# A cached attention decode on one core: three additions of a pair's weighing become one sum over eight tiles

## The chip, the cores and the metric

The kernel runs on one core of a Trainium2 chip. The metric is the device time of one execution in microseconds (us). The engines are called as in the profile: PE is TensorE, PEld its weight loads, DVE is VectorE, ACT is ScalarE, POOL is GpSimd, SP is the engine that issues nearly all transfers.

## The reference

Two layers of the same kind run one after the other, for a batch of two with one token each (D = 448). A layer is an attention over a cache and a gated feed-forward network, each behind a layer norm and with a residual. All data is float32.

```python
def _A_ref(x, k_cache, v_cache, wq, wo):     # B 2, H 16, Sk 4096, Dh 256
    q = (x @ wq).reshape(B, Sq, H, Dh).transpose(0, 2, 1, 3)
    scores = jnp.einsum("bhqd,bhkd->bhqk", q, k_cache) * (Dh ** -0.5)
    p = _softmax(scores, axis=-1)
    o = jnp.einsum("bhqk,bhkd->bhqd", p, v_cache)
    return o.transpose(0, 2, 1, 3).reshape(B, Sq, H * Dh) @ wo

x = x + _A_ref(_layernorm(x, axis=-1), A_k_cache, A_v_cache, A_wq, A_wo)
x = x + _B_ref(_layernorm(x, axis=-1), B_W_gate, B_W_up, B_W_down)
x = x + _A_ref(_layernorm(x, axis=-1), A_k_cache, A_v_cache, A_wq, A_wo)
x = x + _B_ref(_layernorm(x, axis=-1), B_W_gate, B_W_up, B_W_down)
```

## The kernel before

A *pair* is one head of one batch entry. There are 32 pairs in a layer, numbered u = 0 to 31, and the second layer goes through them backwards. A pair has 4 MB of keys and 4 MB of values. One large buffer in SBUF, `arena`, holds three pairs, the head weights and, later, the feed-forward weights. Most pairs come as one transfer of 8 MB for keys and values together; the first few and the last few of a phase come in pieces. The query and output weights of three heads come as one transfer ahead of every sixth pair.

All these transfers are issued by SP in a fixed order, from a list called `pending`. When the program releases a piece of the buffer (`release`), `pump` issues the next transfers of the list for which the buffer has room. A transfer therefore waits for the work that last used its place: an 8 MB transfer for the value tiles of the pair three before it, a weights transfer for the output projection of a head. SP's queue is in order, so a transfer that waits holds up those behind it.

For a pair u the work goes as follows.

- `score` (L379): PE multiplies the keys with the query, 32 matmuls into one of two PSUM banks, `raw`.
- `score_copy` (L387): DVE copies the scores to `found_s`; `score_turn` (L392): PE turns them with four transposes.
- `softmax_max` (L397, L399): DVE takes the maximum over each partition, POOL over all partitions. `softmax_exp` (L404, L407): ACT makes the probabilities `probs`, POOL adds up their sums (L411).
- For most pairs (u = 0 to 28 in the first layer, 5 to 28 in the second, 53 in all) the values are weighed on DVE and ACT. `weigh_rows` multiplies 24 of the 32 value tiles of 256 columns with their probabilities in one DVE instruction (L462); ACT does the other eight (L466). `fold` (L456) then adds the upper half of the tiles to the lower half, in place: 16 tiles, then 8, 4, 2 and 1, the last into `row`. The other pairs are weighed by PE (L439, L430).
- `out_turn` (L486): PE adds `row` over the partitions and scales it with `ri` (L415). ACT copies the result to `oT`, and `project` (L279) multiplies it with the output weights. `query` (L337) makes the query of the next head.

The order of the DVE instructions is the order of the program. `scores_beside(u)` writes out how the scores of pair u and the end of the weighing of pair u - 1 interleave: before, the additions of 16 and 8 tiles stand in `weigh_rows`, right behind the multiplication; that of 4 tiles stands behind the copy of the next scores; those of 2 and 1 stand behind the maximum. After the last one, the value tiles of pair u - 1 are released, and with them the place of a further pair.

Of the kernel before, what the change touches and what calls it, by code (L numbers as in the profile page):

```python
# [11 lines left out]
AX = mybir.AxisListType  # L12
RED = bass_isa.ReduceOp

B, D, H, S, DH, F = 2, 448, 16, 4096, 256, 1792
# [74 lines left out]
def two_layers(  # L90
# [10 lines left out]
    nc = tc.nc  # L101
# [63 lines left out]
    def release(*key):  # L165
        units.free |= units.grains(*at_of.pop(key))
        pump()
# [50 lines left out]
    row = consts.tile([P, DH], F32, name="row")  # L218
# [102 lines left out]
    def attention(order, after, by_rows):  # L321
# [53 lines left out]
        def score(u, c):  # L375
            kt = get("k", order[u], c).rearrange("p (g n) -> p g n", g=G)
            half, j = c // 2, c % 2
            for g in range(G):
                nc.tensor.matmul(  # L379
                    raw[u % 2][32 * g : 32 * g + 2, :], q_of[u][:, j, 1 - half : 3 - half],  # L380
                    kt[:, g, :], start=(c == 0), stop=(c == NC - 1),
                )
            if ("k", order[u], c) not in after:
                release("k", order[u], c)

        def score_copy(u):
            nc.vector.tensor_copy(found_s, raw[u % 2])  # L387

        def score_turn(u):
            s = ps_s.tile([P, E, P], F32, name="small")  # L390
            for e in range(E):
                nc.tensor.transpose(s[:, e, :], found_s[:, e * P : (e + 1) * P], ident)  # L392
            s_of[u] = s.rearrange("p e (g r) -> p r e g", g=G)[:, :2]

        def softmax_max(u):
            mx = work.tile([P, 1], F32, name="mx")
            nc.vector.reduce_max(mx, s_of[u], axis=AX.XYZ)  # L397
            mx_of[u] = work.tile([P, 1], F32, name="top")
            nc.gpsimd.partition_all_reduce(mx_of[u], mx, P, RED.max)  # L399

        def softmax_exp(u):
            b = order[u][1]
            nm = work.tile([P, 1], F32, name="nm")
            nc.scalar.activation(nm, mx_of.pop(u), AF.Copy, scale=nsr[:, b : b + 1])  # L404
            p_of[u] = work.tile([P, NT], F32, name="probs")
            rs = work.tile([P, 1], F32, name="rs")
            nc.scalar.activation(  # L407
                p_of[u].rearrange("p (h e g) -> p h e g", h=2, e=E), s_of.pop(u), AF.Exp, bias=nm, scale=sr[:, b : b + 1], accum_out=rs
            )
            r_of[u] = work.tile([P, 1], F32, name="total")  # L410
            nc.gpsimd.partition_all_reduce(r_of[u], rs, P, RED.add)  # L411

        def softmax_sum(u):
            ri = work.tile([P, 1], F32, name="ri")
            nc.vector.reciprocal(ri, r_of[u])  # L415
            if added(u):
                r_of[u] = ri
                return
            r_of[u] = work.tile([P, 2], F32, name="ri2")
            nc.vector.tensor_scalar_mul(r_of[u], lead, ri)  # L420
# [31 lines left out]
        def fold(u, tiles):  # L452
            at = at_of["v", order[u], 0][0]
            v, n = arena[:, at : at + NC * UNIT], tiles * DH
            to = row[:, :DH] if tiles == 1 else v[:, :n]
            nc.vector.tensor_add(to, v[:, :n], v[:, n : 2 * n])  # L456

        def weigh_rows(u):
            at = at_of["v", order[u], 0][0]
            tiles = arena[:, at : at + NC * UNIT].rearrange("p (t d) -> p t d", d=DH)  # L460
            n = NT - BY_ACT
            nc.vector.tensor_mul(  # L462
                tiles[:, :n], tiles[:, :n], p_of[u][:, :n, None].to_broadcast([P, n, DH])
            )
            for t in range(n, NT):
                nc.scalar.activation(  # L466
                    tiles[:, t], tiles[:, t], AF.Copy, scale=p_of[u][:, t : t + 1]
                )
            fold(u, 16)
            fold(u, 8)  # L470

        def out_copy(u):
            nc.scalar.activation(row[:, :DH], po_of[u][:, :DH], AF.Copy, scale=r_of[u][:, 0:1])
# [9 lines left out]
        def out_turn(u):  # L483
            pT_of[u] = ps_s.tile([P, 2], F32, name="small")
            for c in range(2):
                nc.tensor.matmul(  # L486
                    pT_of[u][:, c : c + 1], row[:, c * P : (c + 1) * P],
                    r_of[u] if added(u) else ones,
                    start=True, stop=True,
                )  # L490

        def out_keep(u):
            h, b = order[u]
            if h not in oT_of:
                oT_of[h] = work.tile([P, 2, B], F32, name="oT")
            if added(u):
                nc.scalar.activation(oT_of[h][:, :, b], pT_of.pop(u), AF.Copy)  # L497
            else:
                nc.vector.tensor_copy(oT_of[h][:, :, b], pT_of.pop(u))

        def project(u):
            h = order[u][0]
            if u % 2 == 0:
                return
            wo = get("o", h, 0)
            for c in range(2):
                add(
                    c, oT_of[h][:, c, :], wo[:, c * D : (c + 1) * D],
                    start=(c == 1 and u == 1), stop=(u == n_u - 1),
                )  # L510
            if ("o", h, 0) not in after:
                release("o", h, 0)
            if u == n_u - 1:
                busy(1, 0)
# [11 lines left out]
        def scores_beside(u):  # L526
            for c in range(NC):
                score(u, c)
            score_copy(u)
            fold(u - 1, 4)  # L530
            score_turn(u)
            softmax_max(u)
            fold(u - 1, 2)
            fold(u - 1, 1)
            for c in range(NC):
                release("v", order[u - 1], c)
            softmax_sum(u - 1)
            softmax_exp(u)
            out_turn(u - 1)
            out_keep(u - 1)  # L540
            project(u - 1)

        def scores(u):
            if added(u - 1):
                return scores_beside(u)
            if_pair(score, u, 0)
            if u == 0:
                spread(total)
            if_pair(score, u, 1)
            if_pair(out_turn, u - 1)  # L550
            if_pair(out_keep, u - 1)
            if_pair(score, u, 2)
            if_pair(score, u, 3)
            if_pair(score_copy, u)
            if u == 0:
                busy(1, 0)
            if_pair(project, u - 1)
            if_pair(score_turn, u)
            if u == 0:
                busy(2, 0)  # L560
            if_pair(softmax_max, u)
            if_pair(softmax_exp, u)

        def outputs(u):
            if added(u):
                weigh_rows(u)
                return
            for c in range(NC):
                weigh(u, c)
            softmax_sum(u)  # L570
            out_copy(u)
            out_add(u)
# [9 lines left out]
        u = n_u - 1  # L582
# [171 lines left out]
```

## Time and profile before

| | |
|---|---|
| time, median of 3 runs | 1316.82 us (1315.99 to 1317.57) |
| time of the profiled execution | 1317.03 us |
| its span in the trace | 1315.3 us |
| bytes read from HBM | 561.52 MB, 427 GB/s over the span |
| busy PE / DVE / ACT / POOL | 635.6 / 894.2 / 260.0 / 397.2 us |

The span lies 1.7 us under the time of the same execution. "Busy" counts an engine's own instructions, not its waits. A share of busy time is an average over stages with different limits.

### The profile page before, as it was taken

To read this page: it belongs to the slowest core of one execution; us is meant where nothing else is said; L and a number is where in the kernel's file an instruction comes from. 1 tells how busy PE (TensorE), PEld (TensorE's weight loads), DVE (VectorE), ACT (ScalarE), POOL (GpSimd) and SP (SyncE) were. 2 spreads that over 40 slices of the span, in tenths; PEclk is the share of its full clock that TensorE was granted. 3 is DMA by queue.
4 is the path that set the end of the run, shared out by engine and by line. 5 is a ranking of instruction groups with operands and counts; after the bars stand their busy time and mean duration, and the time that the engine had idled before them with its cause. 6 is when DMAs were issued, how large, how long until landed. Compare 5 with 4: busy or idle time off the path is not lost.

```text
span 1315.3 us, 10328 instructions
## 1 busy us (share of the span) xinstructions
PE 635.6 (48%) x4018; PEld 195.5 (15%) x4018; DVE 894.2 (68%) x588; ACT 260.0 (20%) x765; POOL 397.2 (30%) x134
## 2 busy tenths in 40 slices
PE   5243434443535254344888653442553434344467
PEld 2011111111111011111232111110111011111122
DVE  1868778886888687958201167887788688787811
ACT  1212212112122121212111121221212122121211
POOL 0424424233343242424000032433334244242400
PEclk9676766766567667666899966676767667666699
DMA  9999999999999999999999999999999999999997
GB/s 419 433 423 439 425 435 433 435 431 429 441 433 431 429 437 427 435 433 425 420 410 417 434 436 435 429 431 439 429 435 431 429 433 432 439 427 435 425 420 320
DMA packets 17341, 562.19 MB, mean 427 GB/s; under 512 B 1926, under 2 KB 2060, under 8 KB 5772
## 3 DMA queue, kind: packets, MB, share of 16 engines
q1 hardware_dynamic: 17284, 561.52, 99.3%
q8 instruction: 32, 0.52, 0.2%
q14 instruction: 17, 0.14, 0.0%
q10 hardware_dynamic: 8, 0.01, 0.0%
HBM read 561.52 MB, written 0.00 MB: 427 GB/s over the span
## 4 chain that ended last, share of the span: by engine, by line
DMA 75%; PE 16%; DVE 7%; issue 1%; ACT 0%; POOL 0%; SPq 0%; DVEq 0%; POOLq 0%; ACTq 0%
DMA arena<-in_kv_cache_dram 72%; PE rawb L379 7%; PE rawa L379 5%; DVE arena L456 4%; DMA arena<-in_w_out_dram 2%; DVE found_s L387 2%; DMA arena<-in_w_in_dram 2%; PE poa L439 1%; DVE row L456 1%; DVE arena L462 0%; POOL top L399 0%; PE small L486 0%; PE y L279 0%; PE pob L439 0%; DVE mx L397 0%
## 5 line engine op out<-in xcount | busy, mean ns | idle before, releaser
L456 DVE TENSOR_TENSOR arena<-arena 128x4096 f32<-128x4096 f32 x212 | 457.1, 2156 | 7.7 <-DVE arena L462 0.5
L411 POOL PARTITION_ALL_REDUCE total<-rs x64 | 357.8, 5590 | 63.6 <-ACT probs L407 63.6
L462 DVE TENSOR_TENSOR arena<-arena,probs 128x6144 f32<-128x6144 f32 x53 | 347.6, 6558 | 28.2 <-ACT probs L407 28.1
L379 PE MATMUL rawb<-arena,q_pad 128*2 128x512 f32 x1024 | 174.5, 841 | 249.5 <-DMA arena<-in_kv_cache_dram 249.5
L399 POOL PARTITION_ALL_REDUCE top<-mx x64 | 38.8, 606 | 804.4 <-DVE mx L397 796.2
L379 PE MATMUL rawa<-arena,q_pad 128*2 128x512 f32 x1024 | 171.5, 826 | 200.9 <-DMA arena<-in_kv_cache_dram 200.8
L404 ACT ACTIVATE nm<-top,nsr 128x1 f32<-128x1 f32 x64 | 18.8, 294 | 889.0 <-POOL top L399 889.0
L466 ACT ACTIVATE arena<-arena,probs 128x256 f32<-128x256 f32 x424 | 175.1, 495 | 0.1
L387 DVE COPY found_s<-rawa 128x512 f32<-128x512 f32 x32 | 22.1, 691 | 124.2 <-PE rawa L379 124.2
L379 PEld LDWEIGHTS rawb<-arena,q_pad 128*2 128x2 f32 x1024 | 28.2, 104 | 378.6 <-DMA arena<-in_kv_cache_dram 266.8
L486 PE MATMUL small<-ri,row 128*128 128x1 f32 x212 | 34.6, 267 | 98.8 <-DVE ri L415 97.1
L387 DVE COPY found_s<-rawb 128x512 f32<-128x512 f32 x32 | 22.1, 692 | 80.7 <-PE rawb L379 80.7
L337 PE MATMUL pq<-arena,xs 128*2 128x256 f32 x300 | 76.0, 416 | 0.0
L379 PEld LDWEIGHTS rawa<-arena,q_pad 128*2 128x2 f32 x1024 | 29.2, 104 | 312.4 <-issue 311.1
L392 PE MATMUL small<-ident,found_s 128*128 128x128 f32 x256 | 42.4, 289 | 50.3 <-DVE found_s L387 50.3
L486 PEld LDWEIGHTS small<-ri,row 128*128 128x128 f32 x212 | 31.7, 215 | 109.9 <-issue 107.9
L392 PEld LDWEIGHTS small<-ident,found_s 128*128 128x128 f32 x256 | 27.1, 142 | 110.7 <-DVE found_s L387 108.8
L337 PEld LDWEIGHTS pq<-arena,xs 128*2 128x2 f32 x300 | 27.1, 98 | 37.7 <-issue 17.8
L344 PE MATMUL pq<-ident,row 2*128 2x2 f32 x60 | 9.9, 233 | 35.6 <-ACT row L341 35.6
L439 PE MATMUL poa<-arena,probs 128*2 128x512 f32 x160 | 22.4, 711 | 9.0 <-DMA arena<-in_kv_cache_dram 5.1
L456 DVE TENSOR_TENSOR row<-arena 128x256 f32<-128x256 f32 x53 | 22.5, 425 | 4.0 <-DVE arena L456 0.5
L279 PE MATMUL y<-arena,oT 128*2 128x192 f32 (+1 forms) x256 | 21.8, 384 | 6.8 <-ACT oT L497 6.8
(95 smaller groups left out, 276.6 us busy)
## 6 DMA issues: line engine op xcount, KB each, us to landing
arena<-in_kv_cache_dram SPq DMA_DIRECT2D x8, 4096.0 KB, 37.6
arena<-in_kv_cache_dram SPq DMA_DIRECT2D x16, 1024.0 KB, 8.8
arena<-in_w_first_dram SPq DMA_DIRECT2D x5, 2688.0 KB, 31.5
arena<-in_w_in_dram SPq DMA_DIRECT2D x14, 896.0 KB, 9.2
arena<-in_w_second_dram SPq DMA_DIRECT2D x3, 2688.0 KB, 15.5
arena<-in_w_out_dram SPq DMA_DIRECT2D x4, 896.0 KB, 13.0
arena<-in_w_second_dram SPq DMA_DIRECT2D x2, 1344.0 KB, 32.3
arena<-in_kv_cache_dram SPq DMA_DIRECT2D x4, 512.0 KB, 32.1
```

What stands on the lines that cost most here:

```text
L279: nc.tensor.matmul(bank[at : at + B, : w_h.shape[1]], stat, w_h, **flags)
L337: nc.tensor.matmul(to, xT[:, c, :], w[:, at : at + n], start=(c == 0), stop=(c > FULL))
L379: nc.tensor.matmul(raw[u % 2][32 * g : 32 * g + 2, :], q_of[u][:, j, 1 - half : 3 - half], kt[:, g, :], start=(c == 0), stop=(c == NC - 1),)
L387: nc.vector.tensor_copy(found_s, raw[u % 2])
L392: nc.tensor.transpose(s[:, e, :], found_s[:, e * P : (e + 1) * P], ident)
L399: nc.gpsimd.partition_all_reduce(mx_of[u], mx, P, RED.max)
L411: nc.gpsimd.partition_all_reduce(r_of[u], rs, P, RED.add)
L439: nc.tensor.matmul(po_of[u][32 * t : 32 * t + 2, :], p_of[u][:, n : n + 2], vt[:, 2 * t * DH : (2 * t + 2) * DH], start=(c == 0), stop=(c ...
L456: nc.vector.tensor_add(to, v[:, :n], v[:, n : 2 * n])
L462: nc.vector.tensor_mul(tiles[:, :n], tiles[:, :n], p_of[u][:, :n, None].to_broadcast([P, n, DH]))
L466: nc.scalar.activation(tiles[:, t], tiles[:, t], AF.Copy, scale=p_of[u][:, t : t + 1])
L486: nc.tensor.matmul(pT_of[u][:, c : c + 1], row[:, c * P : (c + 1) * P], r_of[u] if added(u) else ones, start=True, stop=True,)
```

## The change

The additions of 16 tiles stay where they are. The addition of 8 tiles moves out of `weigh_rows` to the place behind the copy of the next scores, where the addition of 4 stood. The additions of 4, 2 and 1 tiles go; in their place, where the additions of 2 and 1 stood, one `reduce_sum` reads the eight tiles that are left, takes the eight values of each column (256 columns, so 1 KB, apart) one after the other, and writes their sum to `row`.

```diff
         def fold(u, tiles):
             at = at_of["v", order[u], 0][0]
             v, n = arena[:, at : at + NC * UNIT], tiles * DH
-            to = row[:, :DH] if tiles == 1 else v[:, :n]
-            nc.vector.tensor_add(to, v[:, :n], v[:, n : 2 * n])
+            if tiles > 1:
+                nc.vector.tensor_add(v[:, :n], v[:, :n], v[:, n : 2 * n])
+                return
+            rest = v[:, : 8 * DH].rearrange("p (t d) -> p d t", d=DH)
+            nc.vector.reduce_sum(row[:, :DH], rest, axis=AX.X)
...
             fold(u, 16)
-            fold(u, 8)
...
             score_copy(u)
-            fold(u - 1, 4)
+            fold(u - 1, 8)
             score_turn(u)
             softmax_max(u)
-            fold(u - 1, 2)
             fold(u - 1, 1)
```

## Rows read from the trace of the kernel before

**Rows 1.** The page: busy time by engine, and DMA's share in 40 slices.
```profile
PE 635.6 (48%) x4018; PEld 195.5 (15%) x4018; DVE 894.2 (68%) x588; ACT 260.0 (20%) x765; POOL 397.2 (30%) x134
DMA  9999999999999999999999999999999999999997
```

**Rows 2.** The chain that ended last, transfers only: start, us, what.
```profile
260.70 29.66 DMA arena<-in_kv_cache_dram
...
298.75 36.71 DMA arena<-in_kv_cache_dram
...
345.27 29.87 DMA arena<-in_kv_cache_dram
...
383.88 29.95 DMA arena<-in_kv_cache_dram
```

**Rows 3.** The timeline of one pair: start, us, engine, line, what [idle before].
```profile
322.25 0.69 DVE L387 COPY found_s<-rawa 128x512 f32<-128x512 f32 x1 [9.53 <-PE rawa L379]
322.85 1.22 DVE L456 TENSOR_TENSOR arena<-arena 128x1024 f32<-128x1024 f32 x1
...
324.90 0.42 DVE L456 TENSOR_TENSOR row<-arena 128x256 f32<-128x256 f32 x1
...
325.39 0.33 SPq L153 DMA_DIRECT2D arena<-in_kv_cache_dram  x1
...
325.89 6.56 DVE L462 TENSOR_TENSOR arena<-arena,probs 128x6144 f32<-128x6144 f32 x1 [0.49 <-ACT probs L407]
...
332.91 6.75 DVE L456 TENSOR_TENSOR arena<-arena 128x4096 f32<-128x4096 f32 x2 [0.46 <-DVE arena L462]
...
342.11 0.69 DVE L387 COPY found_s<-rawb 128x512 f32<-128x512 f32 x1 [2.45 <-PE rawb L379]
```

**Rows 4.** DVE's groups by line and shape: count, busy us, mean ns, idle before.
```profile
L456 DVE TENSOR_TENSOR arena<-arena 128x4096 f32<-128x4096 f32 x53 | 234.5, 4425 | 5.9 <-DVE arena L462 0.5
L456 DVE TENSOR_TENSOR arena<-arena 128x2048 f32<-128x2048 f32 x53 | 121.5, 2292 | 1.8
L456 DVE TENSOR_TENSOR arena<-arena 128x1024 f32<-128x1024 f32 x53 | 64.4, 1216 | 0.0
L456 DVE TENSOR_TENSOR arena<-arena 128x512 f32<-128x512 f32 x53 | 36.7, 692 | 0.0
L456 DVE TENSOR_TENSOR row<-arena 128x256 f32<-128x256 f32 x53 | 22.5, 425 | 4.0 <-DVE arena L456 0.5
L397 DVE TENSOR_REDUCE mx<-small 128x1 f32<-128x32 f32 x64 | 11.8, 185 | 8.7 <-PE small L392 8.7
L415 DVE RECIPROCAL ri<-total 128x1 f32<-128x1 f32 x64 | 10.0, 157 | 11.8 <-POOL total L411 11.8
L230 DVE TENSOR_REDUCE lead<-ident 128x2 f32<-128x8 f32 x1 | 0.2, 166 | 9.9 <-POOL ident masks.py:199 9.9
L235 DVE TENSOR_REDUCE halves<-ident 128x4 f32<-128x8 f32 x1 | 0.2, 157 | 0.0
```

**Rows 5.** The timeline of SP's queue around a weights transfer.
```profile
283.14 0.33 SPq L153 DMA_DIRECT2D arena<-in_w_first_dram  x1
```

**Rows 6.** PE's timeline at the end of the first attention.
```profile
650.46 3.62 PE L439 MATMUL poa<-arena,probs 128*2 128x512 f32 x32 [0.35 <-DMA arena<-in_kv_cache_dram]
...
660.37 0.61 PE L430 MATMUL pob<-arena,probs 128*1 128x256 f32 x8 [0.66 <-DMA arena<-in_kv_cache_dram]
```

**Rows 7.** PE's timeline at the end of the second attention.
```profile
1277.82 6.41 PE L439 MATMUL poa<-arena,probs 128*2 128x512 f32 x32 [4.74 <-DMA arena<-in_kv_cache_dram]
```

**Rows 8.** Windows: us, busy PE, PEld, DVE, ACT, POOL, granted PE clock, DMA share, GB/s.
```profile
640.00:661.00 21.00, 17.25 (x181) 5.44 (x174) 3.65 (x12) 2.14 (x8) 1.50 (x4) 1.00 0.99 412
...
1276.70:1283.40 6.70, 5.58 (x28) 1.05 (x32) 0.00 (x0) 0.00 (x0) 0.00 (x0) 0.50 0.96 394
```

**Rows 9.** Windows with DVE busy and with DVE nearly idle, columns as in 8.
```profile
595.00:605.00 10.00, 3.35 (x18) 0.78 (x22) 9.86 (x3) 1.14 (x4) 3.91 (x1) 0.62 1.00 433
630.00:640.00 10.00, 9.54 (x56) 2.74 (x60) 0.39 (x2) 1.26 (x6) 0.38 (x1) 0.66 1.00 433
```

## The prediction

> **What bounds the kernel now.** I read the page first. DVE is busiest among the engines with 894.2 us, but that is 68% of the span, while the line of the DMA engines stands at 9 or more tenths in all slices but the last [rows 1]. So the first question is not how long DVE works, but whether its work ever keeps the transfers waiting. The chain that ended last answers in part: it goes from one 8 MB transfer to the next, and between two of them through PE's scores, the copy and the additions, to the release that issues the next transfer [rows 2]. Read quickly, this says that the additions lie on the path. They don't, because the chain counts a transfer from its issue, and it was issued early: the transfer issued at 298.75 us landed at 298.75 + 36.71 = 335.46, and the next but one was already issued at 325.39 [rows 2, 3]. At the moment of a release the queue held 335.46 - 325.39 = 10.1 us of unfinished transfer. The least that I found where issue and landing can both be read is at a weights transfer: issued at 283.14, while the pair ahead of it landed at 260.70 + 29.66 = 290.36, that is 7.2 us [rows 2, 5]. SP's queue is in order, so the 8 MB transfer behind it has the same margin. The kernel is bound by its bytes; a release that comes later by less than 7 us costs nothing in the stages where pairs follow each other.
>
> The second question is DVE's own pace. Pairs land some 19.35 us apart: the transfers of 345.27 and 383.88 landed at 375.14 and 413.83, two pairs in 38.69 us [rows 2]. A weights transfer widens that: 290.36 to 335.46 is 45.1 us for two pairs, 6.4 us more, once in six pairs [rows 2]. The next copy waits for PE's scores: DVE was idle for 2.45 us before the copy at 342.11 and for 9.53 before the one at 322.25 [rows 3].
>
> **The change, part by part.** *The additions that go.* Those of 4, 2 and 1 tiles took 1.216 + 0.692 + 0.425 = 2.333 us a pair [rows 4].
>
> *The sum that comes.* It reads 8 x 256 = 2048 values per partition. The two long additions give DVE's rate: (4425 - 2292) / 2048 = 1.042 ns for each column of output [rows 4]. A reduction's fixed part comes from the maximum: 185 ns for 32 values, less 32 x 1.042, is 152 ns [rows 4]. At one value per tick the sum takes 0.152 + 2048 x 1.042 / 1000 = 2.29 us, 0.05 less than what it replaces. That is 53 x 0.05 = 2.6 us of DVE's busy time.
>
> No row shows a long sum over values 1 KB apart. Two short ones read `ident` with steps of 128 and 256 bytes, 8 values each, in 166 and 157 ns; a reciprocal of one value takes 157 [rows 4]. The faster gives no extra cost per value, so the low end is one tick and 2.29 us. The slower gives (166 - 157) / 7 = 1.29 ns a value, or 2.8 us. As they differ by 9 ns between themselves, I let that much again stand as error for the high end: 18 / 7 = 2.57 ns, 5.4 us. I take 2.29: the maximum, too, reads values that lie 128 bytes apart, in PSUM, and needs no more than its 32 ticks [rows 4].
>
> The Trainium skill speaks against this in "Advanced Engine Details and Errata", section "Memory Cachelines": SBUF has lines of 16 bytes, and an access pattern that goes to another line with every value pays a penalty. It gives no size for VectorE. If the penalty were one more tick for each value, the sum would take 4.4 us; by what follows the time would still come out within the same 0.2%. The trace's short strided reductions show no such penalty, and nothing here tests the rule at 1 KB.
>
> *The move.* Measured from the start of the copy, the last addition ended at 324.90 + 0.42 - 322.25 = 3.07 us [rows 3]. After the change the copy gives way after 0.60 us (322.85 - 322.25), the addition of 8 tiles takes 2.29, the maximum adds some 0.03 (it fits into the gap: from the start of the addition of 4 tiles to that of 2 is 1.25 us for 1.22), and the sum 2.29. That ends at 5.21, so `row`, the release and the transfer behind it come 2.1 us later, or x - 0.15 for a sum of x us. Queued behind the sum on DVE are the reciprocal and the next multiplication; waiting for it are PE's `out_turn`, behind which stand `project`, `query` and the next scores, and SP's next transfer. The margin of 10.1 becomes 8.0, that of 7.2 becomes 5.1. Both still cover it.
>
> The maximum comes later too, by the 1.07 us that 8 tiles take longer than 4. POOL, ACT's probabilities and the multiplication hang on it. In the row the multiplication started 3.64 us after the copy, 0.49 of it in wait for the probabilities [rows 3]. These would now be there at 3.64 + 1.07 = 4.7, before the sum and the reciprocal are done at about 5.35. So the wait of 0.49 goes and the sum takes its place: the multiplication starts 1.7 us later.
>
> From there the addition of 8 tiles is gone. The multiplication started at 325.89 and the addition of 16 tiles at 332.91; it ends 4.43 later, 11.45 us after the multiplication's start [rows 3, 4]. The last work before the next copy thus ends at 5.35 + 11.45 = 16.8 us. The next copy falls 19.35 us after this one, when PE's scores are as quick, so 2.55 us of idle time are left (4.84 - x). Before, it was 2.45 in this row. DVE keeps pace, nothing accumulates from pair to pair.
>
> *Where the margin is smaller.* At the ends of the two attentions the last additions (u = 28) stand before a chain of PE work. In the first layer PE runs from there nearly without a break to 650.46. It then waits five times for values that land, 0.35 us the first time and 0.66 the last, 2.55 us together, the last piece at 660.37 [rows 6]. A delay of 2.1 us fits into these waits with 0.4 to spare, so the attention ends when it did. In the second layer PE waits 4.74 us for its values at 1277.82 alone [rows 7]. It fits there too. At x = 4.4 the first layer's attention would end 4.25 - 2.55 = 1.7 us late at most, which is the most that a doubled sum could cost.
>
> *The sum:* -2.6 us of DVE time, hidden by transfers; +2.1 us on each release, hidden by 5.1 us or more of queued transfer; +2.1 at each attention's end, hidden by waits of 2.55 and 4.74. Total 0 on the execution of 1317.03 us (span 1315.3 and 1.7 around it), which is 0.2 above the median of the runs shown. I forecast 1317.0 us. By how the runs shown differ, about 0.2%, 2.6 us, is what a measurement of this kernel can tell from no change.
>
> **The rivals.**
>
> *The sum is dear and DVE becomes the bound* (slower). With a weights transfer's 6.4 us spread over six pairs, the mean pace leaves room until x = 4.84 + 6.4 / 6 = 5.9 us. From there each further us costs 53. At three ticks a value, x = 0.15 + 3 x 2.133 = 6.55 us: 53 x 0.65 = 34, with the queue's margin nearly used up by the later release (7.2 - 6.4), so some 30 us and 1347. Between 4.9 and 5.9 some pairs run late and a few us are lost, about 1321. For it: the step of 1 KB is unlike any row, and the high end above reaches 5.4. The rule on memory lines named above would work in this way. Against it: the short strided reductions [rows 4]. I give 7 in 100 to a sum over 5.9 and 2 to the stretch below it.
>
> *The end keeps its clock* (faster). After 4.74 us without data PE began the last pair but one at a granted clock of 0.50, the level of 1.2 GHz, and its 32 matmuls took 6.41 us; the same 32 took 3.62 in the stretch granted 1.00, 2.4 GHz [rows 6 to 8]. They free the places of the feed-forward weights. PE's work before that wait moves later, and the wait shrinks. If the clock stayed up, up to 6.41 - 3.62 = 2.8 us come back: 1314.2. Against it: PE's stretch before is delayed by 2.1 us at most and the idle time stays over 2.6 us. 5 in 100. The reverse, PE at the low level for longer at the end of the first attention, has the same price and a spare of 0.4 us: 2 in 100 for over 2.6 us.
>
> *The transfers slow down* (slower). If DVE's steps of 1 KB disturbed the writes into SBUF, each 1% of rate would cost 13 us: 1330. Against it: with DVE busy for 9.86 us of 10 the rate was 433 GB/s, and with 0.39 of 10 it was 433 as well [rows 9]. 1 in 100.
>
> **How the numbers follow.** The hidden change gets 83 in 100, a dear sum 7 + 2, the clock 5 and 2, the transfers 1. That gives faster 5, same 83, slower 12. Within the hidden case the runs shown spread over 1.6 us and a doubled sum adds up to 1.7, so its range is 1315 to 1319; I carry it down to 1314.2 for the clock, and leave the dear sum out above.
>
> **What the profile after would show.** The `reduce_sum` at 2.29 us (up to 5.4); DVE's busy time lower by about 2.6 us; the end of `row` 5.2 us after the copy instead of 3.07; the wait of the multiplication for `probs` gone; DVE still idle before most copies; DMA at 9 tenths in the same slices and 561.52 MB in the same time. The prediction is wrong if DVE shows no idle time before the copy, if transfers are issued less than a us or two before the queue runs dry, or if the sum takes over 4.9 us.

## The result and the profile after

The changed kernel takes 1317.70 us in the median of 22 runs (1316.02 to 1322.75), the kernel before 1315.99 in 22 runs beside it. The ratio is 1.0014 (95% interval 1.0008 to 1.0021): slower by 1.7 us, small but clear of zero. The profiled execution took 1318.64 us, with a span of 1316.9.

The page of the changed kernel: busy time by engine, DMA's share in 40 slices, bytes.

```profile
PE 686.5 (52%) x4018; PEld 219.3 (17%) x4018; DVE 956.7 (73%) x482; ACT 262.0 (20%) x765; POOL 60.4 (5%) x134
...
DMA  9999999999999999999999999999999999999998
...
HBM read 561.52 MB, written 0.00 MB: 426 GB/s over the span
```

The same bytes pass in almost the same time, and DMA's line is as full as before [rows 1]. DVE works 62.5 us longer, not 2.6 shorter. POOL's 397 us have shrunk to 60. The groups of DVE by line and shape say where DVE's time went (count, busy us, mean ns, idle before):

```profile
L465 DVE TENSOR_TENSOR arena<-arena,probs 128x6144 f32<-128x6144 f32 x53 | 346.6, 6540 | 2.8 <-ACT probs L407 2.8
L456 DVE TENSOR_TENSOR arena<-arena 128x4096 f32<-128x4096 f32 x53 | 234.5, 4425 | 5.8 <-DVE arena L465 0.5
L459 DVE TENSOR_REDUCE row<-arena 128x256 f32<-128x2048 f32 x53 | 190.4, 3593 | 0.5 <-DVE mx L397 0.4
L456 DVE TENSOR_TENSOR arena<-arena 128x2048 f32<-128x2048 f32 x53 | 120.9, 2281 | 0.0
```

The sum takes 3.593 us against the 2.333 of the three additions it replaces [rows 4]: 1.26 us more, 53 times. The timeline of one pair, to be laid beside [rows 3]:

```profile
321.59 0.69 DVE L387 COPY found_s<-rawa 128x512 f32<-128x512 f32 x1 [7.30 <-PE rawa L379]
322.19 2.28 DVE L456 TENSOR_TENSOR arena<-arena 128x2048 f32<-128x2048 f32 x1
...
324.58 3.60 DVE L459 TENSOR_REDUCE row<-arena 128x256 f32<-128x2048 f32 x1
...
328.16 6.54 DVE L465 TENSOR_TENSOR arena<-arena,probs 128x6144 f32<-128x6144 f32 x1
328.24 0.33 SPq L153 DMA_DIRECT2D arena<-in_kv_cache_dram  x1
...
334.80 4.42 DVE L456 TENSOR_TENSOR arena<-arena 128x4096 f32<-128x4096 f32 x1
...
341.66 0.69 DVE L387 COPY found_s<-rawb 128x512 f32<-128x512 f32 x1 [2.43 <-PE rawb L379]
```

The row ends 6.59 us after the copy's start (324.58 + 3.60 - 321.59) instead of 3.07, and the next 8 MB transfer is issued behind it. The multiplication no longer waits for the probabilities. DVE is still idle for 2.43 us before the next copy: it keeps pace. So the loss is not DVE's busy time.

What is left is the margin with which transfers are issued. From the chain (start, us, what) and the timeline of SP, around the same weights transfer as in [rows 2, 5]:

```profile
263.50 26.65 DMA arena<-in_kv_cache_dram
```
```profile
285.58 0.33 SPq L153 DMA_DIRECT2D arena<-in_w_first_dram  x1
```

The pair ahead of it landed at 263.50 + 26.65 = 290.15. The weights transfer was issued 4.6 us before that; in the kernel before it was 7.2. That is still more than zero, so by the reading of the prediction it should cost nothing. The experiments ask whether it does. (In this one execution little of the loss lies here: at the fourth weights transfer PE starts on its pair at 536.29 us, before at 536.43.)

### The profile page after: what moved, and what is told of

It reads as the page before. It is cut to its first block, busy times and chain, and to the rows that moved or that the text cites. A ratio compares the mean times of both kernels' runs of the same rounds, so it can differ in the third digit from the quotient of the medians.

```text
span 1316.9 us, 10222 instructions
## 1 busy us (share of the span) xinstructions
PE 686.5 (52%) x4018; PEld 219.3 (17%) x4018; DVE 956.7 (73%) x482; ACT 262.0 (20%) x765; POOL 60.4 (5%) x134
## 4 chain that ended last, share of the span: by engine, by line
DMA 66%; PE 18%; DVE 14%; issue 0%; ACT 0%; SPq 0%; POOL 0%; POOLq 0%; DVEq 0%; ACTq 0%
DMA arena<-in_kv_cache_dram 63%; PE rawb L379 13%; DVE row L459 7%; DVE arena L456 5%; DMA arena<-in_w_out_dram 2%; DVE found_s L387 2%; DMA arena<-in_w_in_dram 2%; PE poa L439 1%; PE rawa L379 1%; PE pob L439 1%; PE pq L337 1%; PE small L392 0%; PE small L488 0%; DVE mx L397 0%; PE poa L270 0%
## 5 line engine op out<-in xcount | busy, mean ns | idle before, releaser
L456 DVE TENSOR_TENSOR arena<-arena 128x4096 f32<-128x4096 f32 x106 | 355.5, 3353 | 5.8 <-DVE arena L465 0.5
L488 PE MATMUL small<-ri,row 128*128 128x1 f32 x212 | 52.1, 350 | 284.6 <-DVE ri L415 284.6
L459 DVE TENSOR_REDUCE row<-arena 128x256 f32<-128x2048 f32 x53 | 190.4, 3593 | 0.5 <-DVE mx L397 0.4
L469 ACT ACTIVATE arena<-arena,probs 128x256 f32<-128x256 f32 x424 | 175.1, 495 | 0.1
L337 PE MATMUL pq<-arena,xs 128*2 128x256 f32 x300 | 102.2, 521 | 0.0
L488 PEld LDWEIGHTS small<-ri,row 128*128 128x128 f32 x212 | 49.2, 322 | 295.6 <-issue 295.6
L399 POOL PARTITION_ALL_REDUCE top<-mx x64 | 22.5, 352 | 1149.5 <-DVE mx L397 1142.9
L499 ACT ACTIVATE oT<-small 128x2 f32<-128x2 f32 x53 | 9.1, 172 | 182.7 <-PE small L488 182.7
L411 POOL PARTITION_ALL_REDUCE total<-rs x64 | 37.2, 581 | 63.5 <-ACT probs L407 63.5
L279 PE MATMUL y<-arena,oT 128*2 128x192 f32 (+1 forms) x256 | 30.5, 519 | 6.8 <-ACT oT L499 6.8
L407 ACT ACTIVATE probs<-small,nm,sr 128x32 f32<-128x32 f32 x64 | 24.1, 377 | 2.1
```

The source lines that it names most:

```text
L279: nc.tensor.matmul(bank[at : at + B, : w_h.shape[1]], stat, w_h, **flags)
L337: nc.tensor.matmul(to, xT[:, c, :], w[:, at : at + n], start=(c == 0), stop=(c > FULL))
L456: nc.vector.tensor_add(v[:, :n], v[:, :n], v[:, n : 2 * n])
L459: nc.vector.reduce_sum(row[:, :DH], rest, axis=AX.X)
L469: nc.scalar.activation(tiles[:, t], tiles[:, t], AF.Copy, scale=p_of[u][:, t : t + 1])
L488: nc.tensor.matmul(pT_of[u][:, c : c + 1], row[:, c * P : (c + 1) * P], r_of[u] if added(u) else ones, start=True, stop=True,)
```

## The experiments

Four theories were open. *The ends*: the later end of pair 28's additions lengthens PE's chains at the close of an attention. *The spread*: each strided sum slows the transfers a little. *Chance*: what PE's clock does in one execution. And, after the first four runs, *the thin margin*: a transfer issued with too little left in the queue costs time although the queue isn't empty. The edits of e1 and e11 are against the kernel before, all others against the changed kernel; "..." stands for lines left out.

**e1, the move alone.**

```diff
             fold(u, 16)
-            fold(u, 8)
...
             score_copy(u)
-            fold(u - 1, 4)
+            fold(u - 1, 8)
             score_turn(u)
             softmax_max(u)
+            fold(u - 1, 4)
             fold(u - 1, 2)
             fold(u - 1, 1)
```

> The addition of 8 tiles moves behind the copy, and the additions of 4, 2 and 1 stand behind the maximum; no sum over strided tiles. The end of the row should come 5.2 us after the copy's start (0.61 + 2.29 + 0.03 + 2.33), against 3.07 before and 6.6 after the change. Theory of the ends (the later end of pair 28's additions lengthens PE's chain at the close of an attention and shifts what its clock does there): between the two kernels, +0 to +1.5 us. Theory of the spread (the strided sum slows the transfers a little in each of the 53 pairs): no change, within 0.5 us of before, as there is no strided sum. Theory of chance (a stretch at PE's low clock at the start of the second attention falls there or not, whatever the additions do): some runs of this kernel lie near before and some about 2 us above it.

Measured: 1315.89 against 1315.82 us, ratio 1.0001 (0.9992 to 1.0010). No loss. The chain and SP's timeline at the same place:

```profile
262.16 28.25 DMA arena<-in_kv_cache_dram
```
```profile
284.85 0.33 SPq L153 DMA_DIRECT2D arena<-in_w_first_dram  x1
```

The margin is 262.16 + 28.25 - 284.85 = 5.6 us.

**e2, the sum alone.** `weigh_rows` keeps the addition of 8 tiles; behind the copy stands nothing; the sum stands behind the maximum.

```diff
             fold(u, 16)
+            fold(u, 8)
...
             score_copy(u)
-            fold(u - 1, 8)
             score_turn(u)
```

> The addition of 8 tiles stays behind the one of 16; only the additions of 4, 2 and 1 become the strided sum, behind the maximum. The sum should take the 3.6 us that it took in the changed kernel, and the row should end about 5.2 us after the copy's start (the maximum waits for PE's transposes until 1.5 us, then 3.6). Theory of the ends: between the two kernels, like the kernel that only moves the addition. Theory of the spread: all of the changed kernel's loss, about +1.9 us, as all 53 strided sums are there. Theory of chance: a mixture as in every variant.

Measured: 1316.11 against 1315.82, ratio 1.0002 (0.9993 to 1.0011). All 53 strided sums are there and nothing is lost, which speaks against the spread. Each half of the change, which brings the row some 2 us later, is free; both together are not.

**e3 and e4, the ends.** e3 gives pair 28 of each layer the additions of before, e4 gives the change to pair 28 alone:

```diff
+        def summed(u):
+            return u != by_rows[-1]        # e4: u == by_rows[-1]
...
```

Pairs for which `summed` is false have the additions of before in their old places, here and in e5, e6, e7 and e9.

> The changed order and sum for all pairs but the last weighed by rows (pair 28 of each layer), which keeps the additions of before in their old places. Theory of the ends: time of before within 0.5 us. Theory of the spread: 51 of 53 sums are left, so +1.8 us. Theory of chance: a mixture, as in every variant.

> The reverse: only pair 28 of each layer has the moved addition and the strided sum, all others keep the additions of before. Theory of the ends: all of the loss, about +1.9 us. Theory of the spread: 2 of 53 sums, so +0.1 us. Theory of chance: a mixture, as in every variant.

Measured: e3 1318.37 against 1315.82, ratio 1.0018 (1.0009 to 1.0026); e4 1316.32, ratio 0.9999 (0.9990 to 1.0008). The theory of the ends falls: the whole loss lies in the other pairs. e2 and e3 together leave a cost that only comes when the row is later than some limit.

**e5, e6, e7 and e9, which pairs cost.** In seven pairs the output projection, which waits for the row, frees the place of a weights transfer; all else in SP's queue stands behind it.

```diff
+        def summed(u):
+            return u not in ((5, 11, 17, 23) if order is first else (9, 15, 21))   # e5
+            return u in ((5, 11, 17, 23) if order is first else (9, 15, 21))       # e6, e9
+            return u in ((6, 12, 18, 24) if order is first else (10, 16, 22))      # e7
...
-            nc.vector.reduce_sum(row[:, :DH], rest, axis=AX.X)
+            for _ in range(2):                                                     # e6, e7
+                nc.vector.reduce_sum(row[:, :DH], rest, axis=AX.X)
...
```

> The changed order and sum for 46 pairs; the seven whose output projection frees the place of the next weights transfer (pairs 5, 11, 17 and 23 of the first layer, 9, 15 and 21 of the second) keep the additions of before. Theory of the thin margin (a transfer that is issued with only some 3 to 4 us left in the queue lets some of the DMA engines run dry before its first packets come; the weights transfer is the one with the least margin, and only its pairs cost time): the loss goes, time of before within 1 us. Theory of the spread (each strided sum slows the transfers a little): 46 of 53 sums are left, so +1.7 to +2.2 us over before.

> Only the same seven pairs have the changed order, and in them the sum is taken twice, so that their row ends 7.0 us later than before (3.6 more than in the changed kernel); all others as before. Theory of the thin margin: the 6 to 7 us of queue that before had at these seven issues are used up, each costs some 2 to 4 us, +14 to +28 us in all. Theory of the spread: 14 sums against the 53 of the changed kernel, +0.5 us.

> The same doubled sum, but in the seven pairs that follow those (6, 12, 18 and 24; 10, 16 and 22), behind whose additions the 8 MB transfer was issued with about 16 us of queue in the kernel before. Theory of the thin margin: 16 less 7 leaves 9 us, so no loss, within 1 us of before. Theory of the spread: +0.5 us. Were DVE's own pace the cause, a pair that lasts 7 us longer would show here as in the other seven: some us each.

> Only the seven pairs ahead of a weights transfer have the changed order and a single strided sum; the other 46 are as before. Theory of the thin margin: the whole loss of the changed kernel, +1 to +2.5 us over before. Theory of the spread: 7 of 53 sums, +0.25 us.

Measured against before: e5 1316.08 to 1316.03 (ratio 1.0001, 0.9992 to 1.0010); e6 1336.19 to 1316.03 (1.0153, 1.0137 to 1.0168); e7 1315.97 to 1316.03 (1.0001, 0.9992 to 1.0011); e9 1318.65 to 1315.78 (1.0021, 1.0012 to 1.0031). So 46 of the 53 pairs carry the change for nothing, and seven carry all of its cost. The same doubled sum costs 20.2 us in these seven, 2.9 us each, and nothing in the seven pairs behind them. Those have even numbers, and no output projection follows an even pair; that a late row with a projection but without a weights transfer is free is shown by e5 alone, for the single sum.

What happens there is plainest in e6. Its timeline at the first of the seven, and four windows (us, busy PE, PEld, DVE, ACT, POOL, granted clock, DMA share, GB/s; a packet counts in the window in which it starts):

```profile
157.27 7.22 DVE L464 TENSOR_REDUCE row<-arena 128x256 f32<-128x2048 f32 x2
...
164.71 0.98 PE L495 MATMUL small<-ri,row 128*128 128x1 f32 x4 [9.02 <-DVE ri L415]
165.73 0.17 ACT L506 ACTIVATE oT<-small 128x2 f32<-128x2 f32 x1 [7.11 <-PE small L495]
...
165.95 1.03 PE L279 MATMUL y<-arena,oT 128*2 128x256 f32 x8 [0.26 <-ACT oT L506]
167.04 0.33 SPq L153 DMA_DIRECT2D arena<-in_w_first_dram  x1
...
167.71 6.35 PE L379 MATMUL rawb<-arena,q_pad 128*2 128x512 f32 x32 [0.73 <-DMA arena<-in_kv_cache_dram]
```
```profile
140.00:165.00 25.00, 7.67 (x43) 2.11 (x41) 19.62 (x9) 2.75 (x9) 5.49 (x3) 0.64 0.98 423
163.00:165.00 2.00, 0.29 (x2) 0.32 (x2) 2.00 (x3) 0.00 (x0) 0.00 (x0) 0.50 0.53 229
165.00:168.00 3.00, 2.00 (x16) 0.82 (x19) 3.00 (x1) 2.27 (x7) 0.00 (x0) 0.50 0.00 0
168.00:171.00 3.00, 3.00 (x16) 0.44 (x12) 3.00 (x1) 1.10 (x3) 0.00 (x0) 0.50 1.05 366
```

From the end of the row it is 2.5 us through `out_turn`, ACT and `project` until SP issues the weights transfer at 167.04. The pair before it has landed, and PE starts on it, at 167.71. For 3 us no packet of data starts. A pair's transfer is spread over the 16 DMA engines, and its packets in the trace show when each is done with it: the first engine at 164.61 us, nine of them by 164.95, the last at 167.22, 0.49 us ahead of PE's start. So at the issue one engine of 16 was still at work. The first packet of the weights begins at 168.00, 0.96 us behind its issue. For all 16 engines to go on without a pause here, the issue would have had to come 0.49 + 2.61 + 0.96 = 4.06 us ahead of PE's start. That is an estimate from this one place; the 2.61 differ from place to place (in e3's trace a pair's engines end 4.2 us apart, from 313.80 to 317.96).

The first packets are slow besides. A weights transfer of 2688 KB goes as 128 packets. In the traces of before, e5, e7 and e11, which issue it 7.0 us or more ahead of PE's start, the usual packet takes 0.80 us and none took over 0.88. With less margin some take up to 2.8 us (e10).

The next table sets the kernels side by side. The margin is the time from a weights transfer's issue to PE's start on the pair ahead of it, the longest packet is the longest of each of the seven transfers; both come from the one profiled execution. The loss is that of the median.

| kernel | margins, first layer; second, us | longest packets, us | profiled execution, us | loss, us |
|---|---|---|---|---|
| before | 8.3, 7.3, 8.4, 8.2; 9.1, 9.0, 9.9 | 0.81 | 1317.03 | |
| e2 | 5.0, 6.5, 6.7, 5.0; 6.0, 5.9, 7.0 | 0.81 to 2.1 | 1315.63 | 0.3 |
| e1 | 5.5, 5.6, 5.7, 5.6; 4.7, 6.3, 5.2 | 0.81 to 2.1 | 1315.41 | 0.1 |
| changed | 4.8, 4.6, 5.6, 4.8; 4.8, 4.7, 5.1 | 1.2 to 2.3 | 1318.64 | 1.7 |
| e9 | 4.3, 4.3, 4.4, 4.6; 5.2, 5.0, 3.9 | 0.81 to 2.5 | 1316.08 | 2.9 |
| e6 | 0.7, 0.5, 0.2, 0.1; 0.6, 0.3, 0.1 | 1.7 to 2.1 | 1336.90 | 20.2 |

Down the rows the margins shrink and, beyond e2 and e1, whose 0.3 and 0.1 lie within the noise, the losses grow. A price of one transfer at one margin can't be read from it: e9's profiled execution is the fastest of its twelve, 0.3 us over the median of before, with margins of 4.3. In e3's trace a weights transfer with a margin of 4.7 us is followed by a pair that comes 27.38 us after the one ahead of it, where 25.84 is the pace before, and one with a margin of 3.6 by a pair at just 25.84. A margin of 3.6 to 5 us thus costs in some executions and not in others, and no run shows what decides it.

**e8, forms of the sum.** Ahead of each pair's sum stands a second one over the same eight tiles, in one of eight forms; its result is used by nothing.

```diff
+            def summed_by(step, per):
+                wide = v[:, : 8 * DH].rearrange("p (a t d) -> p a d t", t=per, d=step)
...
+            if k == 0:
+                out, wide = summed_by(1, 8)
+                nc.vector.reduce_sum(out, wide, axis=AX.X)
...
```

> Ahead of each pair's sum stands a second one over the same eight tiles, in one of eight forms by u modulo 8; its result is used by nothing. Forms: sums of 8 values that lie 4, 8, 16, 64 and 256 bytes apart; sums of 32 values 4 and 256 bytes apart; sums of 2 values 1 KB apart. All read 2048 values. If the distance costs (the rule on memory lines): 2.29 us at 4 and 8 bytes, more from 16 bytes on, 3.6 at 256 bytes whatever the length of a sum. If each finished sum costs (256 of them, 1.31 us, some 5 ns each): 3.6 us for all sums of 8, 2.6 us for sums of 32, 7.5 us for sums of 2. The kernel's time, with a pair some 3.6 us longer than in the changed kernel, is of no use here beyond showing that DVE sets the pace (tens of us more).

Its DVE groups by line and shape. L466, L469, L472, L475 and L478 sum 8 values that lie 4, 8, 16, 64 and 256 bytes apart; L481 and L484 sum 32 values 4 and 256 bytes apart; L487 sums 2 values 1 KB apart; L489 is the sum of the kernel.

```profile
L489 DVE TENSOR_REDUCE row<-arena 128x256 f32<-128x2048 f32 x53 | 189.8, 3581 | 0.0
...
L472 DVE TENSOR_REDUCE arena<-arena 128x256 f32<-128x2048 f32 x7 | 26.4, 3775 | 0.0
L478 DVE TENSOR_REDUCE arena<-arena 128x256 f32<-128x2048 f32 x7 | 25.2, 3594 | 0.0
L475 DVE TENSOR_REDUCE arena<-arena 128x256 f32<-128x2048 f32 x7 | 25.0, 3566 | 0.0
...
L484 DVE TENSOR_REDUCE arena<-arena 128x64 f32<-128x2048 f32 x6 | 21.4, 3572 | 0.0
L466 DVE TENSOR_REDUCE arena<-arena 128x256 f32<-128x2048 f32 x7 | 16.0, 2286 | 0.0
L469 DVE TENSOR_REDUCE arena<-arena 128x256 f32<-128x2048 f32 x7 | 16.0, 2285 | 0.0
L487 DVE TENSOR_REDUCE arena<-arena 128x1024 f32<-128x2048 f32 x6 | 13.8, 2308 | 0.0
L481 DVE TENSOR_REDUCE arena<-arena 128x64 f32<-128x2048 f32 x6 | 13.7, 2286 | 0.0
```

The price goes by the distance, not by the number of finished sums: 2.29 us at 4 and 8 bytes for sums of 8 and of 32, 3.57 to 3.78 from 16 bytes on. The sums of two values 1 KB apart are the exception, at 2.31. The kernel's time was 1363.93 us, one run. With some 3 us more in each pair DVE has little or no idle time left before most copies, and its weights transfers come late too (0.6 us of margin at the first), so this time prices neither.

**e10, the changed kernel again; e11, the end of before filled.** e11 puts nine matmuls on the identity into the wait at the end of the second attention:

```diff
         softmax_exp(u)
+        if order is second:
+            busy(9, 0)
         outputs(u - 1)
```

> The changed kernel once more, on the chip of the other two and with a second profile. Theory of the thin margin: +1 to +2.5 us over before, and in the profile the transfers fall behind those of before by 0 to 1 us at each of the seven weights transfers and nowhere else in the stretches where pairs follow each other; the stretch at PE's low clock at the start of the second attention may be there or not.

> The kernel before with nine more matmuls on the identity (their result is used by nothing) in the wait of 4.74 us for the last values of the second attention. If PE's low clock behind that wait costs the end, as in the profile of before: the 32 matmuls behind it take 3.6 us instead of 6.4, and the kernel is 1 to 2 us faster. If that stretch was an accident of the profiled execution, or the transfers behind it set the end anyway: within 0.5 us of before.

Measured against 1315.78 us of before: e10 1318.39, ratio 1.0017 (1.0008 to 1.0025); e11 1315.65, ratio 0.9999 (0.9990 to 1.0008). e10's profiled execution was its fastest, 1317.02, and bears the theory out only in part: at the four transfers of the first layer its pairs are not late against before, and in the second layer they go from 0.4 us early (PE's start at 875.77 against 876.19) to 1.15 late (1123.57 against 1122.42). In e11's timeline of PE the matmuls behind the wait take the 3.62 us that they take at a granted clock of 1.00, against 6.41 in [rows 7]:

```profile
1276.86 3.62 PE L439 MATMUL poa<-arena,probs 128*2 128x512 f32 x32 [0.75 <-DMA arena<-in_kv_cache_dram]
```

The time hardly moves (the interval goes from -1.3 to +1.1 us). The low clock there is no accident of one execution: in e7 and e9, which have the end of before, the same matmuls took 6.05 and 6.12 us. In the changed kernel PE comes to them without a wait:

```profile
1276.01 3.62 PE L379 MATMUL rawb<-arena,q_pad 128*2 128x512 f32 x32
...
1281.03 3.61 PE L439 MATMUL poa<-arena,probs 128*2 128x512 f32 x32
```

e10 has 3.62 there. The clock is kept and the time doesn't fall, so there is nothing to gain there, and no run here is clearly faster than the kernel before.

The other stretch at the low clock is at the start of the second attention. The window from 688.5 to 695.2 in the changed kernel, in e5 and in e10:

```profile
688.50:695.20 6.70, 6.70 (x29) 3.14 (x32) 0.27 (x2) 0.38 (x2) 0.00 (x0) 0.50 0.63 260
```
```profile
688.50:695.20 6.70, 6.70 (x28) 2.91 (x31) 0.46 (x3) 0.61 (x2) 0.00 (x0) 0.51 0.67 259
```
```profile
688.50:695.20 6.70, 6.70 (x53) 2.72 (x52) 0.94 (x5) 1.75 (x3) 0.00 (x0) 1.00 0.95 364
```

At a granted clock of 0.5 DMA stands at 260 GB/s, against 364. In these traces the executions with this stretch are later behind it: PE starts on a pair at 756.59 us in the changed kernel and at 756.34 in e5, on the same pair at 755.35 before and at 755.22 in e10, and e5's profiled execution, at 1317.98, was the slowest of its eleven. It is not what separates the medians: e5 has it in its profile and the time of before in its median, and e10 and e3 lose 2.6 us in the median and show a granted clock of 1.00 in this window. How often it falls in each kernel is not on record. Comparing the changed kernel's one trace with that of before alone would have ended in the wrong place.

## Why the prediction was right or wrong

**What bounds the kernel** was right: bytes, not DVE. DVE worked 62 us longer and stayed idle before the copies, and 46 of the 53 pairs carry their part of it for nothing (e5). e7, with rows 7 us later for nothing, shows it again. (The 8 MB transfer issued at 325.39 us is the next behind that of 298.75, not the next but one; the 10.1 us stand.)

**The price of the sum** was the first step that failed. The prediction worked out 2.29 to 5.4 us and took 2.29, because the maximum's strided values in PSUM cost one tick each and two short sums over `ident` showed little. It took 3.59. e8 shows that the distance is the reason: from 16 bytes on a value costs (3.593 - 0.152) / 2048 = 1.68 ns instead of 1.042. Eight values were too few to read that from: the row of 157 ns (L235) sums two values each, the form that e8 finds free, and only that of 166 (L230) sums four. The maximum was a poor witness, as the fixed part of 152 ns had been worked out from it at one tick a value; whether PSUM differs no run tests. The rule of the Trainium skill that was set against it ("Advanced Engine Details and Errata", "Memory Cachelines") is borne out by e8 for sums of 8 and 32 values, with the step at just its 16 bytes. The sums of two values, which also change the line with every value, don't pay (2.31 us).

**What follows from x** held once x is put right. With 3.59 the prediction's own terms give an end of the row at 6.5 us (measured 6.59) and a multiplication at 6.65 (6.57). The idle time before the copy came out longer, 2.43 instead of 4.84 - 3.59 = 1.25: the two copies of that row lie 20.07 us apart and not 19.35, and the pause of 0.46 us between multiplication and addition [rows 3] has shrunk to 0.10.

**The margin** was the second step that failed: "a release that comes later by less than 7 us costs nothing". The margin was read rightly, and the right transfer was named as the one with the least. But the sum spent it down to zero, and the signs of being wrong asked for only "a us or two" in reserve. The runs show that more is needed: with margins of 4.7 us and more, most over 5, the medians lose nothing (e1, e2), with 4.6 to 5.6 they lose 1.7 us (the changed kernel), with 3.9 to 5.2 they lose 2.9 (e9), and with under 1 us they lose 2.9 for each of the seven (e6). With x at 2.29 the row would have come some 2 us later, as in e1 and e2, which lost nothing. The two steps together are worth 0.13%, and that they stayed within the 0.2% is luck: nothing in the prediction limited them to it. So is the number 1317.0, only 0.7 us from the 1317.70 measured. It was the one profiled execution of before, 1.0 us over the median of 22 runs, and this hides more than half of the 1.7 us that the change cost.

**The ends of the attentions** cost nothing, as forecast (e4), but not by the terms given. The delay was put at 2.1 us; in the changed kernel's trace the last pair's scores at the end of the second attention start at 1276.01 us, 8.0 later than before. PE waits 5.33 us for the sum of pair 28 instead of 1.83, and `query` and the values of the next pair, which PE does behind this wait, take 3.57 and 5.36 us instead of 1.89 and 3.62. The wait of 4.74 us [rows 7] is used up.

**The rivals**: the dear sum came half way, to 3.59, below the 4.9 from which DVE would set the pace, and it costs by another route. The end kept its clock in both profiles of the changed kernel, and the 2.8 us did not come back; e11 keeps it too and shows that they aren't to be had there. The 53 sums alone lose nothing that could be measured (e2), so the transfers don't slow down while they run.

Why several us have to be queued is seen in e6's packets: the 16 engines end a pair up to 2.6 us apart there, a new transfer's first packet begins 0.96 us behind its issue, and its first packets are slow. What stays open is why an execution with margins of 4 to 5 us loses 3 us or more at one time and nothing at another (e9 ran from 1316.08 to 1322.47), so the 1.7 us of the changed kernel are put down to the seven transfers by the medians of e5 and e9, and not followed transfer by transfer.

## What to carry to other kernels

In a kernel bound by transfers, a later release can cost before the queue is empty: find the transfer that is issued with the least left in the queue, and test what margin it needs by delaying that one alone. On this evidence, a sum of eight or more values that lie 16 bytes or more apart in SBUF is to be priced from a row of the same kind, not from a short one or from PSUM. Differences of one or two us between two single traces can be the clock's; move the suspected part by itself, look at the medians, and ask whether the profiled execution is a usual one.

## What the runs showed of the hardware

- VectorE's sum over SBUF in float32: 1.04 ns a value at distances of 4 and 8 bytes, 1.67 to 1.77 from 16 bytes to 1 KB, and 1.05 for pairs of values 1 KB apart (e8).
- POOL's busy time fell from 397.2 to 60.4 us though POOL does the same work. Its two groups in the changed kernel:

```profile
L411 POOL PARTITION_ALL_REDUCE total<-rs x64 | 37.2, 581 | 63.5 <-ACT probs L407 63.5
L399 POOL PARTITION_ALL_REDUCE top<-mx x64 | 22.5, 352 | 1149.5 <-DVE mx L397 1142.9 <-DVE ri L415 6.6
```

The sum of the probabilities took 5.59 us in the mean before, when it ran beside the multiplication, and takes 0.58 beside the strided sum. The Trainium skill ("SBUF — State Buffer", "Who interferes with whom") says that a DVE instruction with two inputs in SBUF holds up GpSimd's reads, and one with a single input doesn't; the trace agrees. In the pairs weighed by rows nothing waited for that sum, so it gave no time.
- With a transfer issued 0.7 us before PE started on the one ahead of it, no packet of data started for 3 us, and in the 6 us from 165 to 171 the 16 engines moved 183 GB/s (e6). The first packet began 0.96 us behind the issue. The packets of a weights transfer took at most 0.88 us when it was issued 7 us ahead or more, and up to 2.8 us with less.
